# Other places and times for a sum matrix, a weight load, a spectrum, seven power records and dK's quarters in a fused SSM-convolution and MLP gradient kernel

## The chip, the cores and the metric

The kernel runs on one core of a Trainium2 chip. A core has a matrix engine (PE in the profile, with its weight loads as PEld), a vector engine (DVE), a scalar engine (ACT), GpSimd (POOL) and SyncE (SP). The first four compute; SP, POOL and ACT also issue DMA transfers, each on a queue of its own: q1 is SP's, q0 is POOL's, q10 is ACT's. An engine works through its instructions in the order of the program and stops at the first one whose inputs, or whose destination, are not ready. The metric is the device time of one execution in microseconds (us); less is better.

## The reference, cut to what matters

```python
def _A_ref(u, A_re, A_im, B_re, B_im, C_re, C_im, log_dt, Dskip):   # L 2048, D 448, N 256
    dt = jnp.exp(log_dt)[:, None]
    logdA = dt * (A_re + 1j * A_im)
    P = jnp.exp(logdA[:, :, None] * l[None, None, :])
    K = jnp.einsum("dn,dnl,dn->dl", Cc, P, dt * Bc).real
    # y = causal convolution of u with K by rfft2/irfft2 of length 2 L
    return y + u * Dskip[None, None, :]
def _B_ref(x, w1, b1, w2, b2):                                      # F 1792
    h = jnp.einsum("bsd,df->bsf", x, w1) + b1
    r = jnp.where(h > 0, h, 0)
    return jnp.einsum("bsf,fd->bsd", r * r, w2) + b2
g = _sigmoid((x * gate_w).sum(-1, keepdims=True))
out = g * _A_ref(...) + (1 - g) * _B_ref(...)
# returned: out and the gradients of all inputs but B_x, for a given grad_out
```

Forward and backward are one program. The positions l are rounded to bf16, so that many of the 2048 positions share one value; the gradient dK is first summed over the positions that share a value.

## The kernel before, in words

The order of every engine's work is written out by hand. Until about 150 us a list of tokens (FRONT, lines 712 to 722, read by `front`) runs the forward transforms of u (number 0) and of g times grad_out (number 1), and the products that lead to dK:

- `L..` loads a quarter of a transform (line 266). `F..` makes a quarter of a spectrum from it in four parts, and POOL stores the quarter to `sp_d` for a later stage (`spectrum`, line 631). Number and quarter are the digits: the last one is (1, 3).
- `P..` multiplies two spectrum quarters on DVE (line 637). `I..` transforms such a product back on PE; SP stores the result, 448 KB each, to the DRAM tensor `hd` (line 328). `I30a` and `I31s` are the last two.
- `a` and `b` are steps of `powers`: twelve squarings on DVE and ACT, seven chunks of channels at a time. They leave seven records of 1792 columns (448 KB) each, in `Fv` and `w2v` for `a` and in the first 12544 columns of `RB` for `b`, and POOL stores them to `rec_d` (line 606). The store of `b` is one transfer of 3136 KB, at the end of `b20`.
- `r0 r1` load two records back (lines 611, 612), for the tables below. `w1` loads the first layer's weights into the second half of `KW` (lines 706, 708). `Kw` loads the sum matrix `Ew` (line 411) on ACT's queue into the tile `M8`, in which the matrix `M2` lies that every `F` uses.

Then comes the stage of the sums (lines 1153 to 1230):

- SP loads four quarters of dK's transform from `hd`, 896 KB each (line 1156), into parts of `RB`, `KW`, `KW` and `Pt`. Every quarter reads rows of all eight stores of `hd`. Then it loads the second layer's weights `w2n`.
- POOL writes constants into the table buffers (`ends_x`, `ends_y`, lines 806 to 812). `Ys[1]`, the second chunk's, is the second half of `RB`, so it overlaps the records.
- 116 small matmuls (line 1193) multiply columns of `Ew` with the quarters, one quarter after the other, and sum into six PSUM banks. ACT copies these out (line 1201), SP and POOL store them to `dk_d` (lines 1205, 1207), and load them again in another layout as `DK` into `KW[:, 0:7168]` (line 1210: three transfers to even rows on SP, three to odd rows on POOL).
- Meanwhile DVE builds the tables of powers of chunk 0 and chunk 1 (`tables`, lines 745 to 763). `turn_y` transposes chunk 0's table on PE, and ACT copies it from PSUM to `YT`, the first half of `RB` (line 1178). `kgen` (822), `k_out` (829) and `k_add` (836) make the first part of K.
- `D_(n)` brings the dense layers to their n-th step, in between. A step of the first layer is eight matmuls (993, 996) for a pair of blocks, two Relu on ACT into a buffer `rx` (1000), its store to `rT_d` by POOL (1001), and a Square (1002).
- `scale_v(0)` (863) scales `DK` on DVE into `DKc`; `back_z` (877) multiplies `DKc` with `YT`.

After that the list FIRST (1231) handles chunk 1 and builds chunk 2's tables, SECOND the next, and PERIOD the others, up to about 515 us. `+XS +X0 ...` are table steps of the next chunk, `V0` is `scale_v(0)`, `Z P S` the backward steps of the chunk before, and each `D` a share of the dense steps. The rest of the program makes the gradients of the weights and parameters, and the outputs.

Of the kernel before, what the change touches and what calls it, by code (L numbers as in the profile page):

```python
# [349 lines left out]
def kernel(ctx, tc, A_u, A_A_re, A_A_im, A_B_re, A_B_im, A_C_re, A_C_im, A_log_dt, A_Dskip,  # L350
# [54 lines left out]
    def load_const(nm, q):  # L405
# [4 lines left out]
        ct[nm] = K.t("M8", [P, 4096])[:, 0:arr.shape[1]] if nm in ("M2", "Ew") else const.tile([P, arr.shape[1]], bf16, name=f"cb_{nm}")  # L410
# [158 lines left out]
    def powers(c0, homes, cur, sqr):  # L569
# [35 lines left out]
        for a, m, r in R:  # L605
            G_.dma_start(bass.AP(tensor=rec_d, offset=(c0 + a) * P * RS, ap=[[RS, P], [P * RS, m], [1, RS]]), r.rearrange("p c k t w -> p c (k t w)"))
        yield
# [17 lines left out]
    def spectrum(w, q, mode):  # L625
        sp = spw[w, q]
        for ii in range(4):
            K.fwd2_part(s1w[w, q], q, sp, ii, mode)
            if ii < 3:
                yield  # L630
        G_.dma_start(bass.AP(tensor=sp_d[w], offset=q * 4 * 2 * D, ap=[[16 * 2 * D, P], [1, 8 * D]]), sp.rearrange("p a r d -> p (a r d)"))
        yield

# [13 lines left out]
    pows = [powers(0, ((Fv, 4), (w2v, 3)), *fields), powers(7, ((RB, 7),), *fields)]  # L647
# [6 lines left out]
    def front(tok):  # L654
# [33 lines left out]
        elif name[0] == "a" or name[0] == "b":  # L688
            for _ in range(n):
                next(pows["ab".index(name[0])], None)  # L690
# [12 lines left out]
        elif name == "Kw":  # L703
            load_const("Ew", nc.scalar)
# [9 lines left out]
        F10s a1 F10s a1 F10s a1 F10s L12 B0a B1v a1 F11s B2a B3v a1 F11s B4a B5v a1 F11s B6a B7v a1 F11s L13 L02 L03 a1""".split()  # L714
    for tok in FRONT:
# [3 lines left out]
        F02s b1 F02s I10a F02s b1 I11a F02s b1 F12s F12s P20 a20 b1 F12s F12s P21 b1 b1 F03s I20a F03s b1 b1 F03s I21a F03s b1 w1 r0 r1  # L719
        F13s F13s P30 b1 F13s F13s P31 b1 I30a b1 b20 I31s Kw""".split()  # L720
# [487 lines left out]
    for p0, n, r0 in ((0, 24, 0), (50, 16, 24), (82, 16, 24)):  # L1208
        for w in range(2):
            (G_ if w else nc.sync).dma_start(DK[p0 + w:p0 + 2 * n:2], bass.AP(tensor=dk_d, offset=16 * r0 * D, ap=[[16 * D, n], [D, 16], [1, D]]))  # L1210
# [528 lines left out]
```

## Time and profile before

| what | us |
|---|---|
| median of 3 runs | 763.04 (762.24 to 764.33) |
| the profiled execution, its own time | 759.12 |
| its span, first to last instruction | 757.3 |
| PE busy | 585.9 (77%) |
| DVE busy | 577.7 (76%) |
| ACT busy | 461.0 (61%) |
| POOL busy | 147.1 (19%) |
| DMA | 178.99 MB, 236 GB/s on average |

Busy time is counted per engine; no engine is busy all the time, so the waits decide. Times within the program are counted from the span's start. In the timeline a row gives start, busy time, engine, line, operation, what is written and read, how many, and in brackets the idle time before it with its releaser. In the windows a row gives, after the stretch, the busy time of each engine, the granted clock of PE (1.00 is full), the busy share of the 16 DMA engines, and GB/s. In the DMA view a queue has packets, MB and share of the 16 engines, and an issue has the size of one transfer and the time from issue to landing, which is only known for POOL's.

### The profile page before, as it was taken

To read this page: it belongs to the slowest core of one execution; us is meant where nothing else is said; L and a number is where in the kernel's file an instruction comes from. 1 tells how busy PE (TensorE), PEld (TensorE's weight loads), DVE (VectorE), ACT (ScalarE), POOL (GpSimd) and SP (SyncE) were. 2 spreads that over 40 slices of the span, in tenths; PEclk is the share of its full clock that TensorE was granted. 3 is DMA by queue.
4 is the path that set the end of the run, shared out by engine and by line. 5 is a ranking of instruction groups with operands and counts; after the bars stand their busy time and mean duration, and the time that the engine had idled before them with its cause. 6 is when DMAs were issued, how large, how long until landed. Compare 5 with 4: busy or idle time off the path is not lost. (4 is left out here: it accounts for less than half of the span.)

```text
span 757.3 us, 15406 instructions
## 1 busy us (share of the span) xinstructions
PE 585.9 (77%) x6077; PEld 279.8 (37%) x6077; DVE 577.7 (76%) x965; ACT 461.0 (61%) x750; POOL 147.1 (19%) x258
## 2 busy tenths in 40 slices
PE   2676684627599989988978798977687787989886
PEld 0133331203334434445333344435344343445333
DVE  1996888787193999969898899995496957875356
ACT  2886896844458685967626453636666775464453
POOL 1420101312212222211110010011242311232012
PEclk9975575777599999999999999999999999999999
DMA  9998577799669499798998999995699999999862
GB/s 189 294 249 296 205 289 292 225 342 366 145 123 188 121 212 200 167 177 201 210 278 169 281 211 224 178 247 151 216 314 386 271 342 287 320 293 326 218 180 72
DMA packets 194080, 178.99 MB, mean 236 GB/s; under 512 B 128202, under 2 KB 174310, under 8 KB 193382
## 3 DMA queue, kind: packets, MB, share of 16 engines
q1 hardware_dynamic: 174456, 114.74, 60.2%
q0 software_dynamic: 17632, 60.30, 24.4%
q10 hardware_dynamic: 1920, 2.98, 1.6%
q8 instruction: 47, 0.77, 0.4%
q14 instruction: 25, 0.20, 0.1%
HBM read 83.90 MB, written 67.53 MB: 200 GB/s over the span
## 5 line engine op out<-in xcount | busy, mean ns | idle before, releaser
L879 ACT CAST P<-psF 128x1024 bf16<-128x1024 f32 x56 | 56.8, 1013 | 27.5 <-PE psF L877 25.1
L745 DVE TENSOR_TENSOR F<-X,F 128x512 bf16<-128x512 bf16 (+2 forms) x84 | 61.8, 776 | 3.3 <-ACT F L785 2.4
L962 PEld LDWEIGHTS <-U 128*128 128x128 bf16 x448 | 40.7, 101 | 50.4 <-issue 19.8
L1291 PEld LDWEIGHTS <-S 128*128 128x128 bf16 x416 | 39.5, 100 | 40.5 <-issue 10.7
L962 PE MATMUL psN<-S,U 128*128 128x448 bf16 x224 | 50.5, 371 | 1.8 <-DVE U L1059 1.0
L1291 PE MATMUL psX<-D,S 128*128 128x449 bf16 x224 | 50.0, 369 | 2.5 <-DVE S L1280 1.4
L966 ACT CAST D<-psN 128x448 bf16<-128x448 f32 x32 | 17.0, 531 | 56.1 <-PE psN L962 56.1
L967 POOL DMA_DIRECT2D br_d<-D x32 | 17.7, 553 | 165.5 <-ACT D L966 156.7
L890 DVE TENSOR_TENSOR M<-P,psX 128x2048 bf16<-128x2048 bf16 x27 | 32.8, 1215 | 20.5 <-ACT P L879 11.6
L962 PE MATMUL psN<-D,U 128*128 128x448 bf16 x224 | 48.3, 359 | 0.0
L877 PE MATMUL psF<-R,S 114*32 114x512 bf16 x448 | 35.2, 388 | 15.4 <-ACT P L879 9.1
L1055 ACT ACTIVATE U<-psN 128x512 bf16<-128x512 f32 x56 | 30.3, 595 | 21.3 <-PE psN L1052 20.6
L1282 ACT ACTIVATE S<-psN 128x1024 bf16<-128x1024 bf16 x32 | 32.9, 1029 | 15.7 <-PE psN L1278 15.4
L1291 PE MATMUL psX<-K,S 128*128 128x448 bf16 x192 | 41.3, 359 | 1.5 <-ACT S L1294 1.5
L1049 PE MATMUL psN<-S,K 128*128 128x512 bf16 x168 | 41.2, 381 | 0.7 <-issue 0.7
L993 PE MATMUL psN<-S,K 128*128 128x512 bf16 x138 | 35.8, 396 | 1.2 <-issue 0.7
L746 DVE TENSOR_TENSOR X<-F 128x512 bf16<-128x512 bf16 (+2 forms) x42 | 32.8, 781 | 1.4
L891 DVE TENSOR_TENSOR P<-P,psX 128x2048 bf16<-128x2048 bf16 x27 | 33.0, 1221 | 0.9
L850 PE MATMUL psX<-ident,X 128*128 128x128 bf16 x216 | 18.6, 236 | 15.4 <-DVE P L891 13.9
L1280 DVE COPY S<-psS 128x1024 bf16<-128x1024 bf16 x14 | 9.6, 685 | 27.4 <-PE psS L1278 27.1
L1278 PEld LDWEIGHTS <-S 128*128 128x128 bf16 x416 | 26.1, 99 | 10.8 <-issue 5.0
L595 ACT ACTIVATE P<-R 128x896 f32<-128x896 f32 x20 | 19.7, 986 | 12.0 <-DVE R L592 7.4
(378 smaller groups left out, 1456.6 us busy)
## 6 DMA issues: line engine op xcount, KB each, us to landing
hd<-st SPq DMA_DIRECT2D x21, 448.0 KB
sp<-K POOLq DMA_DIRECT2D x8, 896.0 KB, 8.0
dhT_d<-U SPq DMA_DIRECT2D x28, 256.0 KB
R<-sp SPq DMA_DIRECT2D x8, 896.0 KB
S<-dhT_d POOLq DMA_DIRECT2D x14, 512.0 KB, 6.8
R<-hd SPq DMA_DIRECT2D x16, 448.0 KB
S<-rT_d POOLq DMA_DIRECT2D x12, 512.0 KB, 7.4
D<-rT_d SPq DMA_DIRECT2D x20, 256.0 KB
```

The source lines that it names most:

```text
L745: V.tensor_tensor(out=run(vb, 128 * n * r, [256 * n, 2], [1, 128 * n]), in0=run(lo, 2048 * r, [0, 2], [32, 64], [1, 2 * n]), in1=factor(c, ...
L746: V.tensor_tensor(out=run(lo, 2 * n, [32, 128], [1, 2 * n]), in0=Vt[:, 0:256 * n], in1=run(vb, 320 * n, [128 * n, 2], [-64 * n, 2], [1, 64 ...
L877: T_.matmul(psz[32 * k:32 * k + 32, s_], lhsT=DKc[:, o_ + 32 * k:o_ + 32 * k + 32], rhs=run(YT[0:NR, 0:1], 128 * (8 * g + k), [4096, 2], [ ...
L879: S.copy(zbs[c, g // 2][:, :, :, g % 2], psz[:].rearrange("p s (t n) -> p s t n", t=2))
L890: V.tensor_tensor(out=pr.rearrange("p s t g n -> p s (t g n)"), in0=zv, in1=run(xb, 0, [0, 2], [1, 1024]), op=ALU.mult)
L891: V.tensor_tensor(out=z4, in0=z4, in1=run(xb, 512, [0, 2], [-512, 2], [1, 512]), op=ALU.mult)
L962: T_.matmul(ps[:, 0:D], lhsT=hblk[:, j, P * tt:P * tt + P], rhs=ws[:, j, :], start=(w == 1 and j == 0), stop=(j == FT - 1))
L993: T_.matmul(pss[k][:], lhsT=w1w[:, dt, j * P:j * P + P], rhs=UT[:, dt, 512 * lb:512 * lb + 512], start=(dt == 0), stop=False, skip_group_c ...
L1049: T_.matmul(pss[k][:], lhsT=w2Tw[:, jp, dt, k], rhs=dblk[:, dt], start=(dt == 0), stop=False, skip_group_check=True)
L1055: S.mul(hblk[:, 2 * jp + k], pss[k][:], 2.0)
L1282: S.activation(hn(i)[:, 8 * th:8 * th + 8, :], ps[:], ACT.Square if i < FT else ACT.Copy)
L1291: T_.matmul(ps[:, 0:w], lhsT=hn(i)[:, t, :], rhs=(DB2[:, t, :] if i < FT else U[:, t, 0:w]), start=(t == 0), stop=(t == LT - 1))
```

## The change

- `Ew` gets a home of its own, `SB[:, 8192:11904]`. Its load moves from the end of the tokens, on ACT's queue, to the end of the first list, on SP's queue. In the first layer's first block row (`lb` 0) the Relu buffers `rx` that lay there are replaced: two buffers (`w2v[:, 6272:7296]` and `hv[:, 7168:8192]`) in place of three.
- The load of `w1` moves from behind `F03`'s last part to just behind the product `P21`.
- The store of the spectrum quarter (1, 3) moves from its last `F` to the stage of the sums, when PE passes to the third quarter.
- The store of `b`'s seven records is parted: the last three (`parts` 4) where the whole store was, the first four behind the second dense step, when POOL has issued that step's store.
- The quarters of dK lie in `UB[:, 3584:7168]`, `Pt[:, 0:3584]`, `M8` and `KW[:, 0:3584]`, none of them in the records' part of `RB`.
- `ends_y(1)` comes behind the third dense step. All four parts of `turn_y(0, ...)` come after the sums, with one half of each copied by ACT and the other by DVE, and use six PSUM banks.
- `scale_v(0)` comes right behind `k_add(0)`, ahead of chunk 2's table steps, not in their midst. Dense steps 6 and 7 come ahead of FIRST, which keeps its seven `D`.
- On POOL's queue the three `DK` loads are issued in reverse order.

```diff
-        ct[nm] = K.t("M8", [P, 4096])[:, 0:arr.shape[1]] if nm in ("M2", "Ew") else const.tile(...)
+        ct[nm] = SB[:, 8192:8192 + arr.shape[1]] if nm == "Ew" else K.t("M8", [P, 4096])[:, 0:arr.shape[1]] if nm == "M2" else const.tile(...)
...
+        if len(parts) > 1:
+            yield "done"
+        for m0 in parts[::-1]:
+            for a, m, r in R:
+                m1 = min([x for x in parts if x > m0] + [m])
+                G_.dma_start(bass.AP(tensor=rec_d, offset=(c0 + a + m0) * P * RS, ap=[[RS, P], [P * RS, m1 - m0], [1, RS]]), r[:, m0:m1].rearrange("p c k t w -> p c (k t w)"))
+            yield "done"
...
-        G_.dma_start(bass.AP(tensor=sp_d[w], ...
+        if (w, q) != (1, 3):
+            store_spectrum(w, q)
...
-            load_const("Ew", nc.scalar)
+            load_const("Ew", nc.sync)
...
-        ... F11s L13 L02 L03 a1""".split()
+        ... F11s L13 L02 L03 Kw a1""".split()
...
-        ... P20 a20 b1 F12s F12s P21 b1 b1 F03s I20a F03s b1 b1 F03s I21a F03s b1 w1 r0 r1
-        F13s F13s P30 b1 F13s F13s P31 b1 I30a b1 b20 I31s Kw""".split()
+        ... P20 a20 b1 F12s F12s P21 w1 b1 b1 F03s I20a F03s b1 b1 F03s I21a F03s b1 r0 r1
+        F13s F13s P30 b1 F13s F13s P31 b1 I30a b1 b20 b1 I31s""".split()
...
-        rx = [SB[:, 8192:9216], SB[:, 9216:10240], hv[:, 7168:8192]]
+        rx = [w2v[:, 6272:7296], hv[:, 7168:8192]]
             if lb == 1:
-                rx.append(rr[1])
+                rx = [SB[:, 8192:9216], SB[:, 9216:10240], hv[:, 7168:8192], rr[1]]
...
-    hss = [RB[:, 0:3584], KW[:, 0:3584], KW[:, 3584:7168], Pt[:, 0:3584]]
+    hss = [UB[:, 3584:7168], Pt[:, 0:3584], K.t("M8", [P, 4096])[:, 0:3584], KW[:, 0:3584]]
...
-    for c in range(2):
-        ends_x(c)
-        ends_y(c)
+    ends_x(0)
+    ends_y(0)
+    ends_x(1)
...
+    D_(2)
+    next(pows[1])
     D_(3)
+    ends_y(1)
...
             if x8 // 2 < 3:
                 D_(done + 1)
-            else:
-                for j in (0, 2):
-                    turn_y(0, j, "aa")
+            if x8 // 2 == 2:
+                store_spectrum(1, 3)
...
-        for w in range(2):
-            (G_ if w else nc.sync).dma_start(DK[p0 + w:p0 + 2 * n:2], ...)
+        nc.sync.dma_start(DK[p0:p0 + 2 * n:2], ...)
+    for p0, n, r0 in ((82, 16, 24), (50, 16, 24), (0, 24, 0)):
+        G_.dma_start(DK[p0 + 1:p0 + 2 * n:2], ...)
...
-    for k in range(8):
-        next(t1)
-    for j in (1, 3):
-        turn_y(0, j, "aa")
-    banks[:] = NT[:3]
+    banks[:] = NT
+    for k, j in ((8, 0), (0, 2), (1, 1), (0, 3), (0, None)):
+        for _ in range(k):
+            next(t1)
+        if j is not None:
+            turn_y(0, j, "av")
     kps[0] = kgen(0)
     k_out(0, kps[0])
+    banks[:] = NT[:3]
+    D_(6)
     for _ in t1:
         pass
     load_rec(3, G_)
     k_add(0, kps[0])
+    scale_v(0)
     XTs[0, 0], XTs[0, 1] = turn_x(0, 0), turn_x(0, 1, "N3")
+    D_(7)
     expand(2)
-    FIRST = """D +XS +X0 +X1 +X2 V0 +YS +Y0 +Y1 Z0 D Z1 ...
+    FIRST = """D +XS +X0 +X1 +X2 +YS +Y0 +Y1 Z0 D Z1 ...
```

More of the change, by code (lines that the diff above doesn't have):

```diff
@@ L409, in load_const @@
         dr = cdr[nm]
-        ct[nm] = K.t("M8", [P, 4096])[:, 0:arr.shape[1]] if nm in ("M2", "Ew") else const.tile([P, arr.shape[1]], bf16, name=f"cb_{nm}")
+        ct[nm] = SB[:, 8192:8192 + arr.shape[1]] if nm == "Ew" else K.t("M8", [P, 4096])[:, 0:arr.shape[1]] if nm == "M2" else const.tile([P, arr.shape[1]], bf16, name=f"cb_{nm}")
         q.dma_start(ct[nm][:], dr.ap())
@@ L567, with powers @@
     HCH = NCH // 2
-    def powers(c0, homes, cur, sqr):
+    def powers(c0, homes, cur, sqr, parts=(0,)):
         n = HCH * W2
@@ L604, in powers @@
             yield
-        for a, m, r in R:
-            G_.dma_start(bass.AP(tensor=rec_d, offset=(c0 + a) * P * RS, ap=[[RS, P], [P * RS, m], [1, RS]]), r.rearrange("p c k t w -> p c (k t w)"))
-        yield
+        if len(parts) > 1:
[5 more added lines that the diff above has]
+            yield "done"
     def record(c, q):
@@ L630, in spectrum, with store_spectrum @@
                 yield
-        G_.dma_start(bass.AP(tensor=sp_d[w], offset=q * 4 * 2 * D, ap=[[16 * 2 * D, P], [1, 8 * D]]), sp.rearrange("p a r d -> p (a r d)"))
+        if (w, q) != (1, 3):
+            store_spectrum(w, q)
         yield
+    def store_spectrum(w, q):
+        G_.dma_start(bass.AP(tensor=sp_d[w], offset=q * 4 * 2 * D, ap=[[16 * 2 * D, P], [1, 8 * D]]), spw[w, q].rearrange("p a r d -> p (a r d)"))
     def product_half(q, h):
@@ L646 @@
     fields = [RB[:, 12544 + 1792 * i:14336 + 1792 * i].bitcast(fp32) for i in range(2)], W0[:, 3584:5376].bitcast(fp32)
-    pows = [powers(0, ((Fv, 4), (w2v, 3)), *fields), powers(7, ((RB, 7),), *fields)]
+    pows = [powers(0, ((Fv, 4), (w2v, 3)), *fields), powers(7, ((RB, 7),), *fields, parts=(0, 4))]
     sums = iter(range(LT))
@@ L689, in front @@
             for _ in range(n):
-                next(pows["ab".index(name[0])], None)
+                if next(pows["ab".index(name[0])], None) == "done":
+                    break
         elif name[0] == "L":
@@ L713 @@
         V0a V1a q3 V2a V3a q3 V4s V5s V6s V7s L10 L11 q1 row T0a T1a e8 q1 T2v T3a e8 T4v T5a T6v T7a q1 L00 L01
-        F10s a1 F10s a1 F10s a1 F10s L12 B0a B1v a1 F11s B2a B3v a1 F11s B4a B5v a1 F11s B6a B7v a1 F11s L13 L02 L03 a1""".split()
+        F10s a1 F10s a1 F10s a1 F10s L12 B0a B1v a1 F11s B2a B3v a1 F11s B4a B5v a1 F11s B6a B7v a1 F11s L13 L02 L03 Kw a1""".split()
     for tok in FRONT:
@@ L1208 @@
     for p0, n, r0 in ((0, 24, 0), (50, 16, 24), (82, 16, 24)):
-        for w in range(2):
-            (G_ if w else nc.sync).dma_start(DK[p0 + w:p0 + 2 * n:2], bass.AP(tensor=dk_d, offset=16 * r0 * D, ap=[[16 * D, n], [D, 16], [1, D]]))
+        nc.sync.dma_start(DK[p0:p0 + 2 * n:2], bass.AP(tensor=dk_d, offset=16 * r0 * D, ap=[[16 * D, n], [D, 16], [1, D]]))
+    for p0, n, r0 in ((82, 16, 24), (50, 16, 24), (0, 24, 0)):
+        G_.dma_start(DK[p0 + 1:p0 + 2 * n:2], bass.AP(tensor=dk_d, offset=16 * r0 * D, ap=[[16 * D, n], [D, 16], [1, D]]))
     nc.sync.dma_start(DK[48:50, 0], bass.AP(tensor=dk_d, offset=640 * D, ap=[[0, 2], [1, D]]))
@@ L1228 @@
     k_add(0, kps[0])
+    scale_v(0)
     XTs[0, 0], XTs[0, 1] = turn_x(0, 0), turn_x(0, 1, "N3")
+    D_(7)
     expand(2)
[L1231 removed]
+    FIRST = """D +XS +X0 +X1 +X2 +YS +Y0 +Y1 Z0 D Z1 LA +Y2 P0 D Z2 D Z3 LB LQ +Y3 +Y4 P1 D KM KO S0 K1 D D""".split()
     SECOND = """Z0 D S1 Z1 LA T0 P0 D Z2 D Z3 LB LR FE LQ T1 D P1 D S0 SV KM KO D K1 D""".split()
```

3 lines of the change are left out of this document (1 added, 2 removed).

## The prediction, made before the changed kernel ran

> **What bounds the kernel now.** I read the windows first, then the timelines of the five engines from 120 to 250 us, the DMA queues, and the rows of the lines that the change touches. The chain of waits is no help: its oldest piece lies at 389 us. So the stage is argued from who released whom.
>
> ```profile
> 128.00:138.00 10.00, 5.83 (x34) 2.05 (x35) 6.31 (x11) 10.00 (x17) 0.00 (x0) 0.70 0.15 50
> 147.00:168.00 21.00, 8.76 (x36) 2.94 (x33) 16.11 (x25) 11.24 (x17) 2.41 (x9) 0.83 0.99 366
> 168.00:189.00 21.00, 14.59 (x165) 7.00 (x165) 16.70 (x26) 8.66 (x11) 7.13 (x12) 0.75 0.95 334
> 189.00:206.00 17.00, 7.79 (x181) 6.40 (x181) 1.41 (x5) 7.82 (x15) 5.20 (x9) 0.59 0.77 163
> 206.00:223.00 17.00, 15.43 (x161) 5.65 (x160) 16.59 (x22) 9.73 (x12) 2.59 (x4) 0.91 0.43 97
> 223.00:247.00 24.00, 21.75 (x359) 10.00 (x356) 11.36 (x16) 18.64 (x31) 4.67 (x7) 1.00 0.96 179
> ```
>
> From 147 to 189 us the DMA engines are full (0.99, 0.95). From 189 to 206 DVE works 1.41 us of 17. From 206 on PE works 15.43 of 17 and 21.75 of 24. Between 128 and 138 the DMA engines are almost empty (0.15). The rows behind it:
>
> ```profile
> 149.15 0.99 POOL L606 DMA_DIRECT2D rec_d<-R  x1 [3.41 <-ACT R L599]
> 167.96 0.84 POOL L810 MEMSET R<- 128x896 bf16 x1 [16.44 <-DVE Y L756]
> 168.62 0.33 SPq L1156 DMA_DIRECT2D R<-hd  x1
> 173.44 0.58 PE L1193 MATMUL psN<-R,M 128*32 128x448 bf16 x4 [12.73 <-DMA R<-hd]
> 186.57 0.55 PE L1193 MATMUL psN<-P,M 128*32 128x448 bf16 x4
> 188.74 1.84 ACT L1201 CAST st<-psN 128x448 bf16<-128x448 f32 x4 [0.93 <-PE psN L1193]
> 193.01 2.21 SPq L1210 DMA_DIRECT2D K<-dk_d  x3
> 194.22 0.99 POOL L1210 DMA_DIRECT2D K<-dk_d  x2 [0.19 <-issue]
> DMA to landing us min/median/max: 6.8/9.9/11.1
> 197.73 0.29 DVE L836 TENSOR_TENSOR P<-psX,S 128x128 bf16<-128x128 f32 x1 [12.54 <-ACT S L831]
> 204.52 0.37 PE L850 MATMUL psN<-ident,X 128*128 128x128 bf16 x2 [4.79 <-issue]
> 204.93 0.22 DVE L771 COPY X<-rec 128x128 bf16<-128x128 bf16 x1 [6.77 <-PE psN L850]
> 205.24 0.76 DVE L745 TENSOR_TENSOR F<-X,F 128x512 bf16<-128x512 bf16 x2
> 212.09 1.88 DVE L863 TENSOR_TENSOR S<-K,vw 114x1024 bf16<-114x1024 bf16 x2
> 213.81 0.28 DVE L775 COPY Y<-rec 128x256 bf16<-128x256 bf16 x1
> ```
>
> The store of the seven records (149.15) holds the first quarter's home and Ys[1]. POOL stands at L810 until 167.96, with three Relu stores behind it; SP loads the quarters only from 168.62. PE waits 12.73 us, the sums end at 188.7, and everything from the transposes to k_add (197.73) stands behind them. DVE then loses 6.77 us more to a stall of PE (4.79, released by nothing), which lies within the time in which DK lands: POOL's last load, issued at 194.7, plus the longest landing, 11.1, is 205.8. I take the stall for a companion of these loads.
>
> **The change part by part.**
>
> ```profile
> q0 software_dynamic: 208, 1.49, 88.5%
> q1 hardware_dynamic: 208, 0.19, 13.3%
> rec_d<-R POOLq DMA_DIRECT2D x1, 3136.0 KB, 18.7
> 156.00:166.00 10.00, 3.94 (x14) 1.18 (x13) 9.62 (x13) 6.35 (x9) 0.00 (x0) 0.84 1.02 421
> M<-c_Ew ACTq DMA_DIRECT2D x1, 928.0 KB
> K<-in_B_w_dram SPq DMA_DIRECT2D x1, 1344.0 KB
> K<-in_B_w_dram SPq DMA_DIRECT2D x2, 224.0 KB
> 88.19 0.53 POOL L509 DMA_DIRECT2D DBT_d<-S  x1 [3.25 <-DVE R L596]
> DMA to landing us min/median/max: 2.9/4.6/8.9
> 121.41 0.57 POOL L631 DMA_DIRECT2D sp<-K  x1 [5.28 <-DVE K L231]
> DMA to landing us min/median/max: 4.6/8.0/14.1
> ```
>
> The first two rows are the queues from 160 to 164 us: q0 with the records and q1 with the last stores of `hd` send 208 packets each, of 7.2 KB and 0.9 KB. So `hd`'s stores crawl until the records are gone. The Trainium skill's page "DMA: Bandwidth & Descriptors", section "Queues, rings and completion order", says that an engine goes round its queues packet by packet; these rows agree. If the queues shared by bytes instead, the last `hd` store would land some 3 us sooner than I assume below, and the forecast would be that much lower.
>
> ```profile
> 100.74 0.39 SPq L328 DMA_DIRECT2D hd<-st  x1
> 107.48 0.94 ACT L228 CAST st<-psF 128x896 bf16<-128x896 f32 x1
> 108.00:110.00 2.00, 2.00 (x20) 0.87 (x16) 1.65 (x4) 2.00 (x5) 0.00 (x0) 1.00 0.03 10
> 131.94 6.25 SPq L328 DMA_DIRECT2D hd<-st  x2
> 145.80 0.52 ACT L230 CAST st<-psN 128x448 bf16<-128x448 f32 x1
> ```
>
> *Loads moved ahead.* Ew waits on SP for the last transposed block's store (88.19, at most 8.9 to landing, so 97); the next SP work is a store of `hd` at 100.74. Its 0.95 MB take 2.3 us at 421 GB/s and push that store back; DMA idle time follows (share 0.03 from 108 to 110), and ACT asks for the staging buffer again at 107.48. Cost: 0, up to 1.5 if that cover is short. w1 waits on SP for the spectrum store of 121.41 (DMA goes quiet at 128), issues near 128.5 and needs 4.4 us for its 1.84 MB, inside the empty stretch of the first fence. Behind it on SP is only the `hd` store of 131.9, whose buffer ACT fills again at 145.80. Cost 0. Both take 2.8 MB out of the full stretch, so that only the following lies between the last `hd` store and the quarters.
>
> *Gate of the quarters.* Left from about 151 us: three records (1344 KB, 1.38 MB) and the last store of `hd` (0.46 MB), 1.84 MB at 421 GB/s = 4.4 us, to 155.4; with 1.1 us for landing and wake-up the quarters issue at 156.5, not 168.62.
>
> *Quarters to sums.* After issue some 1.6 us pass until data flow, so from 158.1: four quarters (3.67 MB), the four other records (1.84 MB, issued by POOL behind the second dense step, about 156), three Relu stores (0.79) and a record load (0.46), 6.76 MB at 421 = 16.1 us, to 174.2. The quarters pay for the records that were parted off, which is counted here. The last quarter's sums take 186.57 to 188.7, so they end at 176.3, not 188.7. PE has room: the earlier quarters and two dense steps fit before 174.
>
> *Sums to DK.* Before, from the sums' end to the last landing: 205.8 - 188.7 = 17.1 us. So 193.4. POOL's reversed order sends the two queues to different rows. The trace has no such run. Bounds: 0 (slower not excluded, +1), and -5, if the 1.6 MB that took over 10 us went at the stage's usual rate. I take -2, nearer to the row. DK may now only be loaded when spectrum (1, 3) has left `KW`. POOL issues that store behind the fifth dense step's Relu, about 173.5; with the median landing of 8.0 it is gone at 181.5, where dk_d is ready at 176.3 + 4.3 (188.7 to 193.01) = 180.6. That adds 0.9; with the extremes, 0 to 7. DK has landed at 193.4 - 2 + 0.9 = 192.3.
>
> ```profile
> 195.36 1.74 PE L822 MATMUL psX<-Y,X 128*32 128x57 bf16 x128 [1.11 <-ACT R L1178]
> 204.69 2.76 PE L993 MATMUL psN<-S,K 128*128 128x512 bf16 x6
> 246.72 0.22 DVE L770 COPY X<-rec 128x256 bf16<-128x256 bf16 x1
> ```
>
> *DVE.* Its tables start 3 us sooner (the record loads no longer share with w1), and four copies are added; k_add comes at 185.3 by way of PE and ACT: 9.0 us from the last sums to it before (188.7 to 197.73), in which kgen's 1.74 lie, behind 176.3. So what is late next is DK: scale_v(0), now ahead of the table steps, waits some 7 us with all of chunk 2's tables behind it on DVE, and Z0 on PE.
>
> *The sum.* Before, chunk 2's first multiply starts at 205.24 with 1.72 us of scale_v (212.09 to 213.81) still to come: 206.96. After, it starts 2.3 us behind DK (scale_v 1.72, seeds and wake-up 0.6). Gain = 206.96 - (192.3 + 2.3) = **12.4 us**. From there the order is that of before with two dense steps already done, which I count at 0 though PE is busy there; up to 3 us could come of it (the first of such steps takes 2.76 us and more from 204.69, at a low clock). All later inputs are in DRAM long before, so the shift is carried to the end. Against the profiled execution's 759.12: 746.7. The median of the runs stands 3.9 above that execution, so 763.04 - 12.4 = **750.6**.
>
> **The rivals.**
> - *The engines carry mixed packets more slowly.* At 350 GB/s (between the rows of 366 and 334) the two transfers take 5.3 and 19.3 us, DK lands 4.1 later: gain 8.3, 754.7. For: these are means of the very stage; against: they hold the loads of small pieces that are now over before it, and pauses in which nothing was queued. The Trainium skill's page "DMA: Bandwidth & Descriptors", section "Specifications", gives about 358 GB/s as HBM's share for a core, which by itself would make 754; the 421 over ten microseconds disagrees.
> - *The spectrum store is the new gate.* With 14.1 in place of 8.0 it lands at 187.6, DK 12.8 later (193.01 to 205.8) at 200.4, less 2: gain 6.3, 756.7.
> - *More than forecast.* DK at -5 and the two dense steps' 3 us: gain near 18, 745.
> - *Nothing arrives.* PE's 4.79 us stall may belong to its instruction stream and grow, or a later stage may absorb the shift; it takes a wait of 12 us that no row of 206 to 247 shows. 763.
> - *Slower.* POOL's queue turns into a ring: with two `rx` buffers the fifth step's Relu waits for the third step's store, which stands on q0 behind the four records. If these take the 18.7 us of the whole store, from 156.4 to 175.1, the third step's store lands some 2 us later, and with two dense steps' Relu and stores (an estimate of 3 us) spectrum (1, 3) issues at 180.2 and lands, with 14.1, at 194.3; DK at 207.1, the first multiply at 209.4 against 206.96: 765.4. It decides when DK lands past 204.7. Against it: 18.7 was for 3136 KB amid w1 and Ew, and here it is 1792.
>
> **How the numbers follow.** Forecast (750.6, gains 10 to 16) 0.50; slower engines 0.15; spectrum store 0.10; more 0.13; nothing 0.04; slower 0.08. A measurement tells 0.3%, 2.3 us, from no change. Faster 0.88, the same 0.04, slower 0.08. From 745.0 (DK at -5) to 757.5 (beyond the spectrum store's case) lies about 0.8.
>
> **What would show it.** Right: quarters issued near 156 and first sums near 163; sums over near 176; POOL never idle for 16 us; DVE waiting at L863 (before's number) for DK and not for k_add; chunk 2's first multiply near 194.6; PERIOD's first seeds about 12 us sooner than 246.72. Wrong: quarters after 160 (the `hd` stores still share with something), DK landed later than 198, a longer stall of PE without a releaser, or the shift there at 195 and gone at 247.

## The result: 758.15 us, less than half of the forecast gain

| | before | after |
|---|---|---|
| median of 20 runs each, on the same chip | 764.75 us | 758.15 us |
| lowest to highest | 758.96 to 772.27 | 753.38 to 768.25 |
| ratio, 95% interval | | 0.9926 (0.9899 to 0.9952) |
| the profiled execution, its span | 757.3 | 762.9 |

The ratio is of the fast runs alone, the medians are of all runs. It is worth 5.7 us (3.7 to 7.7), less than half of the forecast gain; the medians are 6.6 us apart. Forecast were 12.4 us and a range of 745.0 to 757.5. The profiled execution of after happens to be a long one of its kind (its own time is 764.66), so times in the trace are counted here from one point that the change doesn't touch: POOL's issue of the last `DBT_d` store, at 88.19 us before and at 90.57 after. "First multiply" is chunk 2's first table step on VectorE behind the stage of the sums; "chunk 3's seeds" are the copies that PERIOD starts with. The "gate of DK" is the time from the last sum to SP's first DK load.

### The profile page after: what moved, and what is told of

The parts are those of the page before. It is cut to its first block, busy times and chain, and to the rows that moved or that the text cites. A ratio compares the mean times of both kernels' runs of the same rounds, so it can differ in the third digit from the quotient of the medians.

```text
span 762.9 us, 15411 instructions
## 1 busy us (share of the span) xinstructions
PE 589.9 (77%) x6077; PEld 281.7 (37%) x6077; DVE 582.2 (76%) x969; ACT 457.5 (60%) x746; POOL 148.3 (19%) x259
## 4 chain that ended last, share of the span: by engine, by line
PE 18%; DMA 14%; DVE 14%; ACT 3%; issue 3%; SPq 2%; POOL 0%; ACTq 0%; POOLq 0%; DVEq 0%
PE psX L1308 5%; DMA R<-hd 4%; PE psN L971 3%; PE psN L1058 3%; DMA hd<-F 2%; DVE F L760 2%; DVE F L754 2%; DVE X L1485 1%; DMA k_d<-P 1%; DMA F<-k_d 1%; DVE P L900 1%; DVE M L899 1%; DMA U<-s_d 1%; DMA S<-DBT_d 1%; DVE U L1068 1%
## 5 line engine op out<-in xcount | busy, mean ns | idle before, releaser
L971 PEld LDWEIGHTS <-U 128*128 128x128 bf16 x448 | 42.4, 104 | 55.7 <-issue 27.6
L971 PE MATMUL psN<-S,U 128*128 128x448 bf16 x224 | 53.4, 388 | 3.0 <-issue 2.0
L971 PE MATMUL psN<-D,U 128*128 128x448 bf16 x224 | 51.6, 376 | 0.0
L1058 PE MATMUL psN<-S,K 128*128 128x512 bf16 x168 | 41.2, 381 | 0.4 <-issue 0.4
L1002 PE MATMUL psN<-S,K 128*128 128x512 bf16 x138 | 33.9, 380 | 1.1 <-issue 0.6
L279 PEld LDWEIGHTS <-M 128*64 128x64 bf16 x192 | 13.2, 131 | 35.6 <-issue 30.4
```

Of the source, the lines that this page charges most:

```text
L971: T_.matmul(ps[:, 0:D], lhsT=hblk[:, j, P * tt:P * tt + P], rhs=ws[:, j, :], start=(w == 1 and j == 0), stop=(j == FT - 1))
L1002: T_.matmul(pss[k][:], lhsT=w1w[:, dt, j * P:j * P + P], rhs=UT[:, dt, 512 * lb:512 * lb + 512], start=(dt == 0), stop=False, skip_group_c ...
L1058: T_.matmul(pss[k][:], lhsT=w2Tw[:, jp, dt, k], rhs=dblk[:, dt], start=(dt == 0), stop=False, skip_group_check=True)
```

## The profile after

The timeline of after, the rows that answer to those of the prediction. The numbers of lines are after's: 1165 loads a quarter (1156 before), 1204 sums, 1220 and 1222 load DK, 872 is `scale_v`, 754 a table multiply, 779 a seed copy, 831 K's generation.

```profile
90.57 0.53 POOL L509 DMA_DIRECT2D DBT_d<-S  x1 [3.25 <-DVE R L596]
112.11 0.91 ACT L228 CAST st<-psF 128x896 bf16<-128x896 f32 x1 [1.79 <-DMA hd<-st]
153.78 0.80 POOL L610 DMA_DIRECT2D rec_d<-R  x1 [6.88 <-ACT R L599]
159.78 0.78 POOL L610 DMA_DIRECT2D rec_d<-R  x1
160.90 0.33 SPq L1165 DMA_DIRECT2D U<-hd  x1
171.27 0.57 PE L1204 MATMUL psN<-U,S 128*32 128x448 bf16 x4 [11.25 <-DMA U<-hd]
181.47 0.58 POOL L640 DMA_DIRECT2D sp<-K  x1
182.50 0.71 PE L1204 MATMUL psF<-K,S 128*32 128x448 bf16 x4
189.61 2.21 SPq L1220 DMA_DIRECT2D K<-dk_d  x3
189.98 0.29 DVE L845 TENSOR_TENSOR P<-psX,S 128x128 bf16<-128x128 f32 x1 [0.21 <-ACT S L840]
190.67 1.60 POOL L1222 DMA_DIRECT2D K<-dk_d  x3 [4.30 <-DMA dk_d<-st]
201.87 1.87 DVE L872 TENSOR_TENSOR S<-K,vw 114x1024 bf16<-114x1024 bf16 x2 [11.60 <-DMA K<-k_d]
204.03 0.76 DVE L754 TENSOR_TENSOR F<-X,F 128x512 bf16<-128x512 bf16 x2
219.26 1.74 PE L831 MATMUL psX<-R,X 128*32 128x57 bf16 x128 [6.00 <-DVE P L900]
245.25 0.22 DVE L779 COPY X<-rec 128x256 bf16<-128x256 bf16 x1
```

The gate has opened as forecast: quarters issue 7.12 us behind the record store (153.78 to 160.90), 19.47 us before. VectorE now waits for DK and not for `k_add`, also as forecast (the releaser `K<-k_d` is the last of SP's loads into DK's tile). But PE waits 11.25 us for the first quarter, and the DK loads are issued 6.4 us behind the sums' last matmul (182.50 + 0.71 to 189.61).

The windows by stage: first before, from the record store to the DK loads, then after, the same four stages and the stretch up to `scale_v` as a fifth. The last three numbers are PE's clock, the share of the DMA engines, GB/s.

```profile
149.15:168.62 19.47, 6.61 (x22) 2.06 (x21) 14.58 (x23) 9.38 (x14) 3.03 (x9) 0.81 0.96 353
168.62:173.44 4.82, 0.00 (x0) 0.00 (x0) 4.67 (x12) 0.00 (x0) 4.53 (x10) 0.50 0.79 250
173.44:189.01 15.57, 14.60 (x165) 7.01 (x165) 11.41 (x14) 8.68 (x11) 1.99 (x3) 0.84 1.03 374
189.01:193.01 4.00, 1.68 (x24) 1.56 (x24) 0.00 (x0) 4.00 (x8) 2.10 (x4) 0.89 0.55 159
```

```profile
153.78:160.90 7.12, 4.33 (x21) 1.54 (x19) 6.96 (x11) 5.82 (x9) 5.34 (x13) 1.00 0.94 337
160.90:171.27 10.37, 0.00 (x0) 0.00 (x0) 10.03 (x14) 3.47 (x5) 2.23 (x5) 0.71 1.01 354
171.27:183.21 11.94, 11.94 (x133) 5.31 (x133) 11.51 (x19) 4.94 (x7) 3.08 (x4) 0.82 1.05 372
183.21:189.61 6.40, 5.43 (x195) 5.02 (x195) 6.37 (x10) 6.18 (x11) 2.11 (x4) 1.00 0.86 321
189.61:201.87 12.26, 5.92 (x40) 2.61 (x37) 0.45 (x2) 6.13 (x11) 4.64 (x7) 0.90 0.83 200
```

Row by row: the gate gives 12.35 us; the wait for the first quarter takes 5.55 back (4.82 to 10.37), the gate of DK 2.40 (4.00 to 6.40), and the sums themselves give 3.63, some 3.2 of it because 32 transposes that stood among them (183.40 to 186.57 before; 165 PE instructions there, 133 after) come later now. From the first quarter on PE is busy for 11.94 us of 11.94: the sums end when the *first* quarter has come and PE has done its work, not when the last one lands. Before, the DMA engines had gaps (share 0.79 and 0.55 in the second and fourth stage); after, they are full from the quarters' issue to the last sum (1.01, 1.05) and at 0.86 in the gate of DK.

The queues of after in the first 2 us behind the quarters' issue, then in the 6 us after that:

```profile
q0 software_dynamic: 142, 0.65, 109.4%
```

```profile
q0 software_dynamic: 167, 1.20, 62.6%
q1 hardware_dynamic: 136, 0.90, 36.5%
```

POOL's queue, which got the four other records 1.1 us before the quarters, has the engines to itself for 2 us. By the packets' sizes in the trace, the first microsecond still goes to two Relu stores issued before them (65 packets of 4 KB), the second to the records (54 of 7 KB). In the next 2 us SP's queue sends 27 packets beside 51, and only then do the two take turns.

## The experiments

All ratios are to before, measured beside it; distances in the traces come from one profiled execution each.

**1. Undo one part of the change at a time.** Four kernels, each the kernel after with one edit. The matrix later:

```diff
-        ... B6a B7v a1 F11s L13 L02 L03 Kw a1""".split()
+        ... B6a B7v a1 F11s L13 L02 L03 a1""".split()
...
-        ... F12s F12s P21 w1 b1 b1 F03s ...
+        ... F12s F12s P21 w1 Kw b1 b1 F03s ...
```

> The sum matrix is loaded behind w1 instead of behind L03; all else as in the changed kernel. Theory: in the changed kernel its load stands on q1 ahead of the first store of hd, so ACT waits for the staging buffer; the stretch from the last transposed block's store to the first record store, 60.96 us before and 63.21 after, comes back to 61.0 within 0.4, ACT's wait for a DMA of hd (1.79) is gone, and the time is some 2.2 us below the changed kernel's (ratio to before 0.990). Rival (the 2.25 us are only chance of that execution): the stretch stays at 63 or the time does not move.

The spectrum early:

```diff
-        if (w, q) != (1, 3):
-            store_spectrum(w, q)
+        store_spectrum(w, q)
...
-            if x8 // 2 == 2:
-                store_spectrum(1, 3)
```

> The spectrum quarter (1, 3) is stored at its last part again; all else as in the changed kernel. Theory: that store is what DK's loads wait for, since it is issued behind the fifth dense step's Relu and holds up dk_d's stores on q0; the stretch from the end of the sums to SP's first DK load, 4.0 us before and 6.4 after, falls to 4.0, POOL's first DK load comes 0.5 us behind it and not 1.1, scale_v starts 2 to 3 us earlier, time 2 to 3 us below the changed kernel's. Its own 0.9 MB fall into a stretch in which the DMA engines are half idle; the quarters' issue moves by less than 1 us. Rival (DK's transfers themselves are the limit): DK is issued earlier but scale_v starts no earlier.

Four records behind the quarters, on SP's queue:

```diff
-                G_.dma_start(bass.AP(tensor=rec_d, ...
+                (nc.sync if m0 == 0 and len(parts) > 1 else G_).dma_start(bass.AP(tensor=rec_d, ...
...
         nc.sync.dma_start(hss[q], bass.AP(tensor=hd[0], ...
+    next(pows[1])
...
-    D_(2)
-    next(pows[1])
     D_(3)
```

> The first four records are stored by SP behind the four quarter loads, on the same queue, instead of by POOL ahead of them; all else as in the changed kernel. Theory: these 1.84 MB on q0 took more than half of the engines while the first quarter was on its way; from the quarters' issue to the first sums, 4.8 us before and 10.4 after, falls to 5 to 6; sums over 3 to 4 us earlier, scale_v 3 us earlier, time 3 us below the changed kernel's, unless the spectrum store, issued earlier by as much, holds DK up. Rival (the late start is the wake-up of SP's queue or small packets of the Relu stores): first sums still 9 us or more behind the issue.

One record store:

```diff
-    pows = [..., powers(7, ((RB, 7),), *fields, parts=(0, 4))]
+    pows = [..., powers(7, ((RB, 7),), *fields, parts=(0,))]
...
-    D_(2)
-    next(pows[1])
     D_(3)
```

> The seven records are stored in one transfer again, where the whole store was before; homes and all else as in the changed kernel. Theory: the last store of hd then shares its way with 3.2 MB and not 1.4; from the record store's issue to the quarters' issue 7.1 becomes 11 to 12 us (19.5 before, with w1 and the sum matrix in the way), but the quarters then have the engines for themselves, 5 us to the first sums, not 10.4; so first sums move by less than 2 us and the split itself is worth next to nothing here: time within 2 us of the changed kernel's. Rival (the split is where the gain comes from): first sums 4 us or more later, time 4 us or more above the changed kernel's.

| us | before | after | matrix later | spectrum early | records behind | one store |
|---|---|---|---|---|---|---|
| `DBT_d` store to record store | 60.96 | 63.21 | 60.26 | 61.54 | 61.58 | 61.65 |
| to the quarters' issue | 19.47 | 7.12 | 7.17 | 7.30 | 7.07 | 3.40 |
| to the first sums | 4.82 | 10.37 | 11.36 | 7.48 | 5.05 | 11.24 |
| the sums | 15.57 | 11.94 | 12.08 | 13.40 | 11.49 | 14.55 |
| to SP's first DK load | 4.00 | 6.40 | 5.98 | 5.44 | 12.57 | 6.54 |
| quarters' issue to DK load, sum of these three | 24.39 | 28.71 | 29.42 | 26.32 | 29.11 | 32.33 |
| chunk 3's seeds behind the `DBT_d` store | 158.53 | 154.68 | 152.52 | 151.18 | 153.55 | 153.99 |
| ratio | 1 | 0.9926 | 0.9881 | 0.9933 | 0.9943 | 0.9987 |
| 95% interval | | 0.9899–0.9952 | 0.9822–0.994 | 0.9888–0.9978 | 0.9903–0.9983 | 0.9939–1.0035 |

The matrix later brought its stretch back, and ScalarE's wait for `hd` is gone. The spectrum early was half a miss: the gate of DK fell to 5.44 us, not to the 4.0 expected, and POOL's first DK load still came 1.1 us behind SP's; the rest of its 2.39 us lies in front, with the first sums 2.89 sooner and the sums 1.46 longer. With the records behind the quarters the first sums came 5.3 us sooner, as expected, and the DK loads still left 29.11 us behind the quarters' issue: what was won in front was lost behind. The time hardly followed any of the three: only the matrix later stands below after, and the intervals overlap. The bytes offer a reason. The windows from the quarters' issue to the DK load of after, of the kernel with the records behind, and of the one with the spectrum early:

```profile
160.90:189.61 28.71, 17.37 (x326) 10.33 (x326) 27.90 (x41) 14.59 (x22) 7.43 (x13) 0.82 0.99 354
```

```profile
157.08:186.19 29.11, 17.81 (x324) 10.93 (x325) 28.07 (x41) 14.69 (x22) 7.38 (x13) 0.76 0.95 349
```

```profile
159.66:185.98 26.32, 16.65 (x195) 9.06 (x196) 25.50 (x38) 13.80 (x21) 7.08 (x13) 0.81 0.97 350
```

The engines are 0.95 to 0.99 busy, and the time goes with the bytes: 28.71 us x 354 GB/s = 10.2 MB, 29.11 x 349 = 10.2 MB, and without the spectrum's 0.92 MB 26.32 x 350 = 9.2 MB. The missing 0.92 MB at 350 GB/s are 2.6 us; the differences are 2.4 and 2.8. One record store is a miss: the quarters were expected 11 to 12 us behind it and came 3.40 behind, because the last store of `hd`, which they wait for, was all but through before the records filled the queue (its packets end at 154.1 us, the records' begin at 153.9). The first sums then came 11.24 us behind the issue, not 5, and the time, expected within 2 us of after's, is 4.7 us above it by the ratios, where the rival had it (4 or more), though the intervals still touch. The trace, which stands like that of after at chunk 3's seeds, doesn't explain it, so what the parting of the store is worth in the time stays open.

**2. The edits together, and PE's idle time in chunk 1.** The first of these kernels moves dense half-steps alone, the others combine it with the edits above.

```diff
-    FIRST = """D +XS ... +Y3 +Y4 P1 D KM KO S0 K1 D D""".split()
+    FIRST = """D +XS ... +Y3 +Y4 P1 D D D KM KO S0 K1""".split()
```

> Edit: the kernel after, with the two dense half-steps at the end of the first chunk's list moved in front of its K generation (three there instead of one). Theory: in the kernel after TensorE idles 6.00 us in front of line 831 for the first chunk, because two half-steps were taken out of this stretch, and it is fully busy from there to chunk 3's seeds; three half-steps of about 1.9 us each fill the idle time, one before, three now, so chunk 3's seeds come 2 to 4 us sooner behind the last DBT_d store than in the kernel after (154.7 us there, 151 to 153 here) with X0 unchanged (113.5 +- 1), and the time is 0.988 to 0.990 of before (0.9926 for the kernel after). Rival: that stretch is set by VectorE and ScalarE and not by TensorE; then the seeds stay at 154 to 156 us, and the ratio at 0.992 to 0.995.

Without that edit, matrix later, spectrum early and records behind:

> Edit: the kernel after with the three edits that were run alone: the sum matrix loaded behind w1, the spectrum (1,3) stored at its last F part, and the first four records stored from SP's queue behind the quarters. Theory: the three losses are separate; DBT store to record store 60.3 us, issue to first sums 5.0, sums 11.5, and the DK loads 4.5 to 6 us behind the sums (12.57 with the records moved alone, since the spectrum's store then stood in front of dk_d's), so scale_v at 100 to 103 us behind the last DBT_d store (111.3 after, 107.1 and 110.2 in the two alone) and X0 at 102 to 105; the ratio to before 0.980 to 0.985. Rival: the 1.8 MB of records that go behind the quarters, and not the spectrum, are what dk_d's stores wait for; then the DK loads stay 9 us or more behind the sums, scale_v is at 105 to 107 and the ratio 0.987 or more.

Matrix later, spectrum early, dense half-steps:

> Edit: the kernel after with the sum matrix behind w1, the spectrum (1,3) stored at its last F part, and the dense half-steps in front of the first chunk's K generation; the records stay as in the kernel after. Theory: the gains of the parts add, 2.6 us at X0 for the matrix and about 3 for the spectrum, and 2 to 4 in the first chunk: X0 at 107 to 109 us, chunk 3's seeds at 146 to 149 us behind the last DBT_d store (113.5 and 154.7 after), ratio to before 0.981 to 0.985. Rival: the seeds of chunk 3 come sooner, but the later chunks are set by loads and dense work that the earlier start doesn't move; the ratio stays at 0.988 or above.

All four:

> Edit: all four, the three of the run before it and the dense half-steps in front of the first chunk's K generation. Theory: another 2 to 4 us on top of the three together: X0 at 102 to 105 us, chunk 3's seeds at 141 to 145 us, ratio to before 0.976 to 0.982. Rival (records behind the quarters hold dk_d): X0 at 106 to 108 us, seeds at 145 to 148, ratio 0.983 to 0.986.

| us | dense steps | three edits | matrix, spectrum, dense | all four |
|---|---|---|---|---|
| to the first sums | 11.23 | 4.95 | 7.39 | 5.00 |
| the sums | 11.92 | 11.59 | 13.44 | 12.20 |
| to SP's first DK load | 6.16 | 9.79 | 5.49 | 9.35 |
| quarters' issue to DK load | 29.31 | 26.33 | 26.32 | 26.55 |
| first multiply behind the `DBT_d` store | 113.57 | 108.49 | 109.66 | 109.60 |
| chunk 3's seeds | 151.72 | 149.72 | 149.38 | 148.74 |
| ratio | 0.991 | 0.9855 | 0.9854 | 0.9818 |
| 95% interval | 0.9871–0.9948 | 0.9801–0.9908 | 0.9812–0.9896 | 0.9764–0.9872 |

The dense half-steps brought chunk 3's seeds 3 us forward, as expected (154.68 to 151.72): their matmuls fill PE's idle time in front of K's generation, and the 6.00 us in front of it are gone. The time, 0.991, is not the 0.988 to 0.990 expected, but its interval holds both and the kernel after too.

```profile
215.08 2.92 PE L971 MATMUL psN<-D,U 128*128 128x448 bf16 x14
217.93 1.35 PE L831 MATMUL psX<-R,X 128*32 128x57 bf16 x128
```

The three edits together went as the rival had it: `scale_v` was expected at 100 to 103 us and stood at 106.32; the ratio, 0.9855, lies between the two forecasts. With the matrix, the spectrum and the dense half-steps the first multiply (109.66), the seeds (149.38) and the ratio (0.9854) stand just beyond the worse ends of the forecast's ranges (109, 149 and 0.985). All four edits missed in the trace, with the first multiply and the seeds later than even the rival's (106 to 108 and 145 to 148), and yet their ratio, 0.9818, is in the range of the theory. Whether the records go in front of the quarters or behind them, the DK loads follow 26.3 to 26.6 us after the quarters' issue, in all four kernels without the spectrum.

**3. Take other bytes out.** The second layer's weights, 1.6 MB behind the quarters on SP's queue, are read by none of the work from the sums to DK. Loaded early, in the second list:

```diff
-    nc.sync.dma_start(w2n, bass.AP(tensor=B_w2.tensor, ...
...
+        elif name == "w2":
+            nc.sync.dma_start(w2v[:, 0:FT * D].rearrange("p (j d) -> p j d", d=D), bass.AP(tensor=B_w2.tensor, ...
...
-        ... I21a F03s b1 r0 r1
+        ... I21a F03s b1 r0 r1 w2
```

> Edit: the kernel after with one more load taken out of the stretch between the record store and the DK loads: the second layer's weights (1.6 MB, line 1167, issued right behind the quarters) are loaded in the second list, behind the two record loads. Theory (bytes): in the runs so far that stretch has the DMA engines busy for 0.9 to 1.05 of the time in every kernel, and lasts as long as its bytes take: 14.54 MB in 43.86 us before, 12.56 in 35.83 after, 11.74 in 33.62 with the spectrum early, 12.54 in 36.18 with the records behind the quarters, 12.54 in 35.73 with one record store. So 1.6 MB less is 4.6 us less: 31 to 32 us from the record store to the first DK load, scale_v at 106 to 108 us behind the last DBT_d store (111.3 after), the ratio to before 0.985 to 0.989. Rival (a chain of landings, of which the second weights are none: quarters, sums, dk_d, DK): the stretch stays at 34.5 to 36 us and the ratio at 0.991 to 0.994. The point that could spoil both: the load delays the inverse transform's stores that follow it on the queue; then the stretch from the DBT_d store to the record store grows by more than 1 us.

With matrix later, spectrum early and dense half-steps, in the two orders of the records:

> Edit: sum matrix behind w1, spectrum (1,3) stored at its last F part, dense half-steps in front of the first chunk's K generation, and the second weights loaded early. Theory (bytes): 11.72 MB in 33.74 us without the second weights' edit, 10.1 MB with it, 29 to 30 us; scale_v at 102 to 104 us behind the last DBT_d store (107.5), chunk 3's seeds at 144 to 146 (149.4), ratio to before 0.978 to 0.982. Rival (chain of landings): 33 us or more, seeds at 148 to 150, ratio 0.984 to 0.987.

> Edit: the same, and the first four records stored from SP's queue behind the quarters. Theory (bytes): the order inside the stretch doesn't matter, only its bytes, so this kernel stands within 1 us of the one with the records as after, in the stretch (29 to 30 us), at chunk 3's seeds and in the ratio (0.978 to 0.982). Rival (chain of landings): the sums end 6 us sooner with the records behind, the DK loads then have less in front of them without the second weights, and this kernel is 2 us or more faster than the other.

And the kernel before with nothing but the first weights moved:

```diff
-        ... F12s P21 b1 b1 F03s ... F03s b1 w1 r0 r1
+        ... F12s P21 w1 b1 b1 F03s ... F03s b1 r0 r1
```

> Edit: the kernel before with nothing of the change but the first layer's weights, loaded behind P21 instead of in front of r0. Theory (bytes): 1.6 MB leave the stretch between record store and DK loads, 14.54 - 1.6 = 12.9 MB, at 331 to 350 GB/s 37 to 39 us (43.86 before, 35.83 after), so that this one edit brings two thirds or more of what the whole change brought there; ratio to before 0.993 to 0.997. Rival (the gate): the quarters still wait for the whole record store to be out of their home; only the part of the store's landing that the weights took goes, under 3 us of the 43.86, and the ratio is 0.997 or more.

The early load went wrong in the way named as its spoiler, only elsewhere. Record store to quarters' issue took 10.67 us alone, 18.93 with the records as after, 13.42 with the records behind (7.1 to 7.6 in the kernels they were built from), because the last `hd` stores stand behind the weights on SP's queue. SP's waits from 125 to 180 us in the second of these kernels (total, times, longest):

```profile
SPq L1166 <- DMA hd<-st: 17.5, 2, 11.6
```

So record store to DK load stayed at 35.82 (expected 31 to 32), rose to 39.59 (expected 29 to 30), and was 34.90 in the third (expected within 1 us of the second). But the gate of DK, with the weights no longer in front of `dk_d`, fell to 4.06, 3.95 and 4.47 us. The ratios are 0.9889 (0.9832 to 0.9945), 0.986 (0.9795 to 0.9925) and 0.9827 (0.9784 to 0.987): no worse than without the edit, and not measurably better.

The first weights alone gave 0.9918 (0.9877 to 0.9959), which can't be told from the whole change. In the trace record store to DK load fell from 43.86 to 39.76 us, half of the 8.03 that the whole change brings there, where two thirds were expected. These weights are 1.84 MB, not the 1.6 of the expectation, so the bytes gave 36 to 38 us, and the rival 40.9 or more: the measured time lies between. Chunk 3's seeds stand at 156.09, 2.4 of the 3.85 us that the whole change brings there.

**4. The same bytes out at the other end.** The second weights behind SP's DK loads, so that they delay nothing in front:

```diff
-    nc.sync.dma_start(w2n, bass.AP(tensor=B_w2.tensor, ...
...
     nc.sync.dma_start(KW[48:50, D:7168], bass.AP(tensor=k_d, ...
+    nc.sync.dma_start(w2n, bass.AP(tensor=B_w2.tensor, ...
```

> Edit: the kernel after with the second layer's weights (1.6 MB, line 1167, issued right behind the quarters) issued behind SP's DK loads instead, so that nothing is put in front of the quarters. Theory (bytes): from the quarters' issue to the first DK load the engines are full, and the time is the bytes over some 350 GB/s, whatever their order: 28.71, 29.42 and 29.11 us in the kernel after, with the matrix later and with four records behind the quarters; 26.32, 26.33, 26.55 and 26.32 in the four kernels from which the spectrum's 0.92 MB had gone. 1.6 MB less is 4.6 us less: 24 to 25 us here, scale_v at 106 to 108 us behind the last DBT_d store (111.3), ratio to before 0.985 to 0.989. Rival (chain of landings: quarters, sums, dk_d, DK; the second weights are none of them): 28 us or more, ratio 0.991 to 0.994. What could spoil the theory's gain: the dense steps read these weights from X0 on; if they land more than 6 us behind it, the gain at X0 is given back before chunk 3's seeds.

> Edit: sum matrix behind w1, spectrum (1,3) stored at its last F part, dense half-steps in front of the first chunk's K generation, second weights behind SP's DK loads. Theory (bytes): from the quarters' issue to the first DK load 21.5 to 22.5 us (26.32 with the weights in front); scale_v at 102 to 104 us behind the last DBT_d store (107.5), chunk 3's seeds at 144 to 147 (149.4), ratio to before 0.978 to 0.982. Rival (chain): 25.5 us or more, seeds at 149, ratio 0.984 to 0.987.

> Edit: the same, and the first four records stored from SP's queue behind the quarters. Theory (bytes): the order of the transfers doesn't matter, so 21.5 to 22.5 us (26.55 with the weights in front) and everything else within 1 us of the run before it. Rival (chain of landings): the sums end 6 us sooner than with the records as after, dk_d's stores now have only the records in front of them, and DK is loaded 2 us or more sooner than there.

Windows from the quarters' issue to the DK load: before; late weights with the records as after (and matrix, spectrum, dense); the same with the records behind.

```profile
168.62:193.01 24.39, 16.28 (x187) 8.56 (x187) 16.08 (x25) 12.68 (x18) 8.62 (x16) 0.78 0.91 314
```

```profile
157.27:184.95 27.68, 15.94 (x192) 8.65 (x193) 26.08 (x38) 12.44 (x19) 6.83 (x12) 0.75 0.77 276
```

```profile
159.26:180.93 21.67, 15.01 (x187) 8.42 (x188) 20.89 (x32) 13.29 (x20) 6.83 (x12) 0.84 0.96 352
```

Here the two theories part. All three carry the same 7.6 to 7.7 MB (24.39 x 314, 27.68 x 276, 21.67 x 352). With the records as after the first quarter still comes after 11.18 us, PE then works 12.43 of 12.48 us, the gate takes 4.02, and the engines idle for a quarter of the time: the chain decides, and taking bytes out bought nothing. With the records behind, the first sums come after 4.86 us, the engines stay full, and DK is loaded 6.0 us sooner. So, as far as these kernels show, the stretch lasts as long as the longer of two: its bytes at some 350 GB/s, or first quarter plus some 12 us of PE plus the gate. In the kernel after the bytes were the longer: 10.2 MB at 350 GB/s are 29 us, and its chain with the 4.13 us gate of the next kernel is 26.4.

The edit alone landed between the two (26.47 us, expected 24 to 25 or 28 and more): the gate fell from 6.40 to 4.13, the rest stayed, and the engines were no longer full (0.88). The late weights were paid for at the dense steps, where PE waited for them in the kernel with the records as after:

```profile
204.39 2.77 PE L970 MATMUL psN<-D,U 128*128 128x448 bf16 x7 [12.95 <-DMA D<-in_B_w_dram]
```

With the records behind, `scale_v` ran at 103.51 us, 7.8 us sooner than after, but the first multiply only at 112.55, behind the next thing in line: ScalarE's scaling of the table's factors, which stands behind a dense step's Relu. That step stood behind a stall of PE, 3.58 us to 195.53, that the trace puts down to nothing; the stall before the change (4.79) looks the same there, and the kernel after has none. Chunk 3's seeds stood at 152.84 and 151.53, later than either forecast for the first of the two.

```profile
202.88 0.76 DVE L753 TENSOR_TENSOR F<-X,F 128x512 bf16<-128x512 bf16 x2 [5.86 <-ACT F L793]
```

The ratios: alone 0.9875 (0.9833 to 0.9917), records as after 0.9861 (0.9811 to 0.991), records behind 0.9785 (0.9735 to 0.9836). The last, 752.88 against 768.96 us, and all four edits of experiment 2, 749.54 against 765.7, have the lowest ratios; their intervals overlap, and both lie wholly below that of the kernel after, as do two others by less (upper bounds 0.987 and 0.9896). They are worth 16.5 and 13.9 us, more than the forecast's 12.4, with the dense half-steps, which the forecast didn't have, among their edits. Chunk 3's seeds account for 7.0 of the 16.5 us (158.53 to 151.53); where the rest comes from the single trace doesn't show.

## Why the prediction was wrong, step by step

| step, us | forecast | measured | difference |
|---|---|---|---|
| `Ew` ahead, in the front | 0 | 63.21 - 60.96 = 2.25 | +2.25 |
| record store to quarters' issue | 156.5 - 149.15 = 7.35 | 7.12 | -0.23 |
| quarters' issue to the sums' end | 176.3 - 156.5 = 19.8 | 10.37 + 11.94 = 22.31 | +2.51 |
| sums' end to DK load | 4.3 + 0.9 = 5.2 | 6.40 | +1.20 |
| DK load to first multiply | 12.8 - 2 + 2.3 = 13.1 | 204.03 - 189.61 = 14.42 | +1.32 |
| first multiply to chunk 3's seeds | 246.72 - 206.96 = 39.76 | 245.25 - 204.03 = 41.22 | +1.46 |

These are 8.5 us of the 12.4. What is left, 3.85 us at chunk 3's seeds (158.53 to 154.68), lies within the measured 3.7 to 7.7.

*Right.* The gate of the quarters, to 0.2 us, and with the `hd` stores sharing with three records as it was worked out; but with one record store the gate was 3.40, so the parting of the store is not what opened it. `w1` hidden in the empty stretch. VectorE waiting for DK, not for `k_add`. POOL without its 16 us of idle time. PE's stall is gone; whether it belonged to the DK loads, as the prediction took it, no run decides.

*The step "quarters to sums" failed, in its mechanism.* It let the sums end with the last quarter's landing, at 6.76 MB and 421 GB/s, and gave PE room to spare. PE had none: its work from the first quarter on took 11.94 us without a gap, so the landing that counted was the first quarter's, and that was delayed by what POOL's queue held in front of it, above all the very records that had been parted off to let the quarters start. The records' bytes were counted; what their place ahead of the first quarter does was not. The five kernels with the records behind the quarters show it: first sums 4.9 to 5.05 us behind the issue, in place of 10.37.

*Its rate and its bytes were off too.* From issue to DK load 10.2 MB moved at 354 GB/s. The forecast took the highest row of the stage, 421 over ten microseconds, and left out of its bytes the second weights (1.6 MB) and the spectrum (0.92 MB), which pass in front of `dk_d`. The first rival, 350 GB/s, had the rate of this stretch, and its time, 754.7, was nearer. That is in part luck: it charged the gate of the quarters too, which came as forecast, and it too waited for the last quarter. The Trainium skill's page "DMA: Bandwidth & Descriptors", section "Specifications", gives about 358 GB/s as a core's share of HBM; the 346 to 354 of the full stretches agree in size. A ceiling it isn't: the sums of the kernel with the records behind ran at 397 GB/s.

*"Sums to DK" was short by 2.5 us.* In the kernels made from after whose records stand in front of the quarters the gate of DK is 4.0 to 4.1 us wherever the second weights are out of the way, with the spectrum early or late; 5.4 to 5.5 with the weights and the spectrum early; 6.0 to 6.5 with both. (Before it was 4.00, with the weights behind the quarters and the spectrum early: the sums took 3.6 us longer there, and the engines were at 0.55 in the gate.) The forecast had 0.9 us for the spectrum, and nothing for the weights, which cost more. The 2 us for POOL's reversed order were never seen: with it, DK load to `scale_v` took 11.4 to 12.9 us in all kernels. POOL's last DK load landed 11.6 us behind SP's first load in after and 10.8 to 12.6 in the others with this order, against 12.9 before and 11.8 with the first weights alone, which have the old one. The order alone wasn't changed in any run.

*"Cost 0" for `Ew` was wrong by about 1 us, inside its own bound of 1.5.* The single difference of 2.25 us overstates it. Over all traces the stretch is 62.38 us on average in the seven kernels with `Ew` early (61.54 to 63.21) and 61.33 in the ten with `Ew` late, before among them (60.26 to 61.82 us). ScalarE waits for an `hd` store in six of the seven, for up to 1.79 us, and in none of the ten. The cover named for it, DMA idle time from 108 to 110 us, came too late: the store was pushed back beyond the point where ScalarE asked for its buffer.

*"From there the order is that of before ... which I count at 0" missed 1.5 us.* Two dense steps fewer in FIRST left PE idle for 6.00 us in front of K's generation, and the work behind it didn't move up. Three half-steps moved there brought 3 us at chunk 3's seeds.

## What to carry to other kernels

When a gate in front of a transfer is opened, sum every byte that then stands between this gate and the next one, the loads that nobody waits for too, at the rate that the stage itself shows; here the stretch lasted as long as its bytes or its chain, whichever was longer, and an edit of the shorter one bought nothing. What counts for a chain of loads that feeds an engine is the first landing plus the engine's work, where the later loads land while it works, so what isn't needed soon goes behind the first load in time, not merely onto another queue. Moving one 1.84 MB load into a stretch in which the engines idle gave, within the runs' spread, as much as the whole rearrangement (0.9918 and 0.9926).

## What the runs showed of the hardware

- Half a microsecond of order went with 3 us of landing. The four records (1792 KB, POOL's queue) issued 0.5 and 0.6 us ahead of the quarters let the first sums start 7.4 to 7.5 us behind the quarters' issue; issued 0.9 to 1.15 us ahead, 10.4 to 11.4 us, in five kernels; behind the quarters on SP's queue, 4.9 to 5.05 us, in five. Issued 1.8 us ahead, in one kernel, it was 8.7, and 11.4 us ahead, in another, 5.1, so it is no simple slope, and no run moved this order alone. In the five kernels with 10.4 to 11.4 us SP's queue sends at most 3 packets in the first 2 us, beside some 140 on POOL's, and its third and fourth issue take 1.5 to 2.1 us each; with the records behind they take 0.4 to 0.7. With one record store, issued 3.4 us ahead, POOL's queue sent 236 packets from 155 to 160 us and SP's none, with its loads issued from 154.66 on. Why the engines leave a queue that was just rung standing for so long, the traces don't tell.
- Once both queues run, they send equal numbers of packets: 58 and 59 from 6 to 8 us behind the issue in after. In the eight microseconds from 150 of the kernel with the early weights and the records as after it was 504 packets with 2.34 MB on POOL's queue and 509 with 0.46 MB on SP's, where the second weights pass in packets of 0.9 KB. What stood behind them waited: SP spent 17.5 us on the `hd` stores in that kernel, 6.3 in after. The Trainium skill's page "DMA: Bandwidth & Descriptors", section "Queues, rings and completion order", has an engine go round its queues packet by packet; these numbers agree, those of the first 4 us behind the issue in after (142 packets to 0, then 51 to 27) do not.
- Runs of one kernel spread over 2% of the time (753.38 to 768.25 us in 20 runs of after), so edits worth less than 3 us in the trace could not be told apart in the time.
